# Half of the first product of blocks 4 to 10 as seven smaller products

## The chip, the cores and the metric

The kernel runs on one core of a Trainium2 chip. The metric is the device time of one execution in microseconds (us), the median over the runs of a kernel. Engines: TensorE (PE) multiplies matrices into PSUM, and PEld is its loading of weights. VectorE (DVE), ScalarE (ACT) and GpSimd (POOL) work on elements. SyncE (SP) issues the DMAs of this kernel, all on one queue.

## The reference

A retention recurrence (RetNet) over 4 batches, 8 heads, 768 steps and a head size of 64, then a feed-forward layer with the activation mish on the 3072 tokens that it gives, 512 wide, 2048 inside:

```python
for t in range(S):
    state = gamma[None, :, None, None] * state + np.einsum('bhd,bhe->bhde', k[:, :, t], v[:, :, t])
    y[:, :, t] = scale * np.einsum('bhd,bhde->bhe', q[:, :, t], state)
...
x = np.ascontiguousarray(y.transpose(0, 2, 1, 3)).reshape(B * S, H * D)
h = x @ w_in
sp = np.where(h > 20.0, h, np.log1p(np.exp(np.minimum(h, 20.0))))
g = h * np.tanh(sp)
out = (g @ w_out).astype(np.float32)
```

Inputs and output are float32. The kernel multiplies in 16-bit floats and adds up in 32 bits.

## The kernel before

**Chunks and blocks.** The tokens are cut into 24 chunks of 128 (6 per batch). Block 0 has four chunks, blocks 1 to 10 have two (256 tokens). A block goes through the recurrence in its chunked form, which gives `xts[blk]`, the transposed x in 16 bits (4 groups of 128 channels by tokens), then through the feed-forward layer.

**First product.** `g1(blk, u)` for u = 0 to 7 makes two of the 16 groups of 128 hidden channels: 2 times 4 matmuls of 128x128 weights (`wins`) against 256 tokens into one PSUM bank, and one `AF.Mish` of 512 elements per partition on ACT into the tile `g` (`gtiles`).

**Second product.** `seven(blk, ...)` multiplies the block's 2x2 parts of g with the 2x2 parts of w_out by seven products instead of eight (Winograd's form of Strassen's scheme). The sums of weights (`tmats`) are made once. `sums_a`, `sums_b` and `sums_c` make the sums of g (`gsums`) on DVE in each block. Each of the seven products is 8 matmuls of 256 columns. ACT copies three results out of PSUM (`snap`), DVE adds the others (`done`) into `osb`, and SP stores `osb`.

**Recurrence beside it.** In the middle of `seven`, the list `hooks[0]` calls `retain(blk + 1, blk + 2)`: PE works on the past part of y for the next block, interleaved with the scores (`at`) and outer products (`u_ps`) of the block after that, in small 64x64 matmuls, in the order of the two streams. `finish` then adds the present part and copies x out of PSUM. `settle` (three DVE steps on the states), `mask_two` (the scores times a triangular mask, on DVE) and `leave` (the state that the next block starts from) follow; in blocks 4 and up they are called after the first unit of the next block's `g1`.

**Feeding the recurrence.** q, k and v of a chunk are loaded by SP (`load_to`, three DMAs), scaled into 16 bits by POOL (`casts`: q and k into one tile, then v), and q and k are turned by a transposing DMA on SP (`turn_by_dma`). From block 3 on `cast_behind` has POOL cast the two chunks of three blocks ahead, one after the other, behind a one-element copy that waits for DVE's sums; `next_two(g, soon)` issues on SP a load, the two transposes (in block 3 both before the second load, `soon`; in later blocks one before and one after it) and a second load. The stores of a block are issued by `store_due` after units 1 and 2 of the next block's `g1`, so behind all of these in SP's order.

**Order.** The order on each engine is written out by hand and every engine runs its own list in order; semaphores hold an instruction until its operands are there and its buffer is free. PSUM has eight banks: three in the pool `mmps`, one in `pxps`, and two tiles of two banks in `atps` that hold `at` and `u_ps`.

Of the kernel before, what the change touches and what calls it, by code (L numbers as in the profile page):

```python
# [9 lines left out]
FP16 = mybir.dt.float16  # L10
FP32 = mybir.dt.float32
AF = mybir.ActivationFunctionType
ALU = mybir.AluOpType
# [3 lines left out]
def kernel(  # L17
# [102 lines left out]
    gtiles, tmats, gsums = {}, [], []  # L120
    ONE = 3
    nload, ncast = [0], [0]
    stores, weight_left = [], []

# [64 lines left out]
    def store_due(now):  # L191
        while stores and stores[0][0] <= now:
            _, dst, osb = stores.pop(0)
            nc.sync.dma_start(dst, osb)
# [165 lines left out]
            nc.vector.tensor_copy(dst, src)  # L360

    def casts(g):
        qf, kf, vf = loaded.pop(g)
        qk16 = castp.tile([P, 2, H, D], FP16, name="qk16", bufs=4)
        q16, k16 = qk16[:, 0], qk16[:, 1]
        v16 = castp.tile([P, H, D], FP16, name="v16", bufs=7)
        heads = slice(g % 2 * (H // 2), (g % 2 + 1) * (H // 2))
        nc.gpsimd.tensor_tensor(  # L368
            q16.rearrange("p (r h) d -> p h r d", r=2), qf,
            qs_two[:, heads].unsqueeze(3).broadcast_to((P, H // 2, 2, D)), op=ALU.mult)  # L370
        nc.gpsimd.tensor_tensor(  # L371
            k16, kf, boosts.unsqueeze(2).broadcast_to((P, H, D)), op=ALU.mult)
        nc.gpsimd.tensor_tensor(  # L373
            v16, vf, vs[g % 2].unsqueeze(2).broadcast_to((P, H, D)), op=ALU.mult)
        cast[g] = (q16, k16, v16, qk16)

    def turn_by_dma(g):
        qkt = qktp.tile([P, H, C], FP16, name="qkt", bufs=6)
        nc.sync.dma_start_transpose(qkt, cast[g][3].rearrange("p a h d -> p (a h d)"))
        qkts[g] = (qkt[:, :HP].rearrange("p (r i) c -> p i r c", r=2), qkt[:, HP:])  # L380

    def cast_to(g):
        while ncast[0] < min(g, NCK):
            casts(ncast[0])
            ncast[0] += 1
# [100 lines left out]
    def settle(blk):  # L486
        a = first[blk]
        u = held[blk][1]
        for j in range(2):
            us[a + j] = u[:, :, j]  # L490
        mid_of(a)
        state_of(a)
        mid_of(a + 1)

    def mask_two(blk):
        at = held.pop(blk)[0]
        am = tpp.tile([P, 2, 2, HP, D], FP16, name="am")
        nc.vector.tensor_tensor(  # L498
            am.rearrange("p a j i c -> p (a j i) c"), at.rearrange("p a j i c -> p (a j i) c"),
            tri_half.rearrange("p r c -> p (r c)").unsqueeze(1).broadcast_to((P, 4 * HP, D)), op=ALU.mult)  # L500
        for j in range(2):
            ams[first[blk] + j] = am[:, :, j]

    def leave(blk):
        state_of(first[blk] + 1)
# [128 lines left out]
    def sums_a(blk, half):  # L634
        n = NFB // 4
        (s1, s2, _, _), a11, _, a21, a22 = sum_views(blk, slice(half * n, (half + 1) * n))
        nc.vector.tensor_tensor(s1, a21, a22, op=ALU.add)  # L637
        nc.vector.tensor_tensor(s2, s1, a11, op=ALU.subtract)
# [5 lines left out]
    def sums_c(blk):  # L644
        (_, s2, _, s4), _, a12, _, _ = sum_views(blk)
        nc.vector.tensor_tensor(s4, a12, s2, op=ALU.subtract)  # L646

    def seven(blk, masks, hooks, last):
        n, hf = NFB // 2, d_model // 2
        px = pxps.tile([P, hf], FP32, name="o_ps", tag="px")  # L650
        pb = mmps.tile([P, hf], FP32, name="o_ps", tag="mm")
        osb = [op.tile([P, d_model], FP32, name="osb", tag="osb") for _ in range(2)]

        def a(i, j):
            return lambda f: gts[blk, j * n + f][:, i * P:(i + 1) * P]

        def b(i, j):
            return lambda f: wouts[(i * n + f) // FPS][:, f % FPS, j * hf:(j + 1) * hf]

        def s(i):  # L660
            return lambda f: gsums[blk % 2][:, i - 1, f]

        def t(i):
            return lambda f: tmats[(i - 1) // 2][:, (i - 1) % 2, f]

        def mm(o_ps, x, w, first=False):
            for f in range(n):
                nc.tensor.matmul(  # L668
                    o_ps, x(f), w(f), start=first and f == 0, stop=f == n - 1,
                    skip_group_check=True)  # L670

        def snap(o_ps):
            x = op.tile([P, hf], FP32, name="snap", tag="snap", bufs=3)
            nc.scalar.copy(x, o_ps)  # L674
            return x

        def done(i, j, o_ps, plus=None):
            dst = osb[i][:, j * hf:(j + 1) * hf]
            if plus is None:
                nc.vector.tensor_copy(dst, o_ps)  # L680
            else:
                nc.vector.tensor_tensor(dst, o_ps, plus, op=ALU.add)  # L682
            if last:
                nc.sync.dma_start(out_rows(blk, i)[:, j * hf:(j + 1) * hf], dst)

        mm(px, a(0, 0), b(0, 0), True)
        m1 = snap(px)
        mm(pb, a(0, 1), b(1, 0), True)
        done(0, 0, pb, m1)
        sums_b(blk)  # L690
        if blk == 1 or not tight(blk):
            cast_behind(blk, 2)
        for fn, *args in masks:
            fn(*args)
        pe = mmps.tile([P, hf], FP32, name="o_ps", tag="mm")
        if last:
            mm(px, s(2), t(2))
            u2 = snap(px)
        mm(pe, s(1), t(1), True)
        m5 = snap(pe)  # L700
        if not last:
            mm(px, s(2), t(2))
            u2 = snap(px)
        for fn, *args in hooks[0]:
            fn(*args)
        sums_c(blk)
        if blk > 1 and tight(blk):
            cast_behind(blk, 3)
        for fn, *args in hooks[1]:
            fn(*args)  # L710
        mm(px, s(3), t(3))
        done(1, 1, px, m5)
        for fn, *args in hooks[2]:
            fn(*args)
        mm(pe, s(4), b(1, 1))
        done(0, 1, pe, u2)
        mm(px, a(1, 1), t(4))
        done(1, 0, px)
        if not last:
            for i in range(2):  # L720
                stores.append((1 + i, out_rows(blk, i), osb[i]))
# [180 lines left out]
    def turn_next(g):  # L902
        if g < NCK:
            cast_to(g + 1)
            turn_by_dma(g)
# [2 lines left out]
        turn_next(g)  # L908
        load_to(g + 3)

    def next_two(g, soon):
        load_to(g + 3)
        turn_next(g)
        if soon:
            turn_next(g + 1)
        load_to(g + 4)
        if not soon:
            turn_next(g + 1)

    def cast_behind(blk, i):  # L920
        g = first[blk] + (6 if blk == 1 else 8)
        if ncast[0] < min(g, NCK):
            nc.gpsimd.tensor_copy(summed, gsums[blk % 2][:, i, NFB // 2 - 1, P - 1:])  # L923
            cast_to(g)

    def tight(blk):

        return blk <= ONE

    def plan_of(blk):  # L930
        a = first[blk] + 4
        plan = {u: [] for u in (0, 1, 4, 5, 7)}
        if tight(blk):
            plan[5] = [(get_ready, blk + 1)]
        elif blk + 1 < len(BLOCKS):
            plan[0] = [(settle, blk + 1), (mask_two, blk + 1), (leave, blk + 1)]
        if blk == 1:
            plan[0] += [(turn_next, a)]
            plan[1] += [(load_to, a + 3)]
        elif blk < ONE:  # L940
            plan[1] += [(next_chunk, a)]
            plan[4] += [(load_to, a + 4)]
        return plan

    first_block()
    for blk in range(1, len(BLOCKS)):
        last = blk + 1 == len(BLOCKS)
        plan = plan_of(blk)
        for u in range(NFB // 2):
            store_due(u)  # L950
            g1(blk, u)
            if u in ((6, 7) if tight(blk) else (5, 7)):
                sums_a(blk, u // 7)
            for fn, *args in plan.get(u, ()):
                fn(*args)
            if weight_left:
                weight_left.pop(0)()
        hooks = [[], [], []]
        if not last:
            later = blk + 2 if ONE <= blk < len(BLOCKS) - 2 else None  # L960
            hooks = [[(retain, blk + 1, later, True)],
                     [(next_two, first[blk] + 6, tight(blk))] if blk >= ONE else
                     [(turn_next, first[blk] + 5), (load_to, first[blk] + 8)] if blk == 1 else
                     [(next_chunk, first[blk] + n) for n in (5, 6, 7)],
                     [(finish, blk + 1)] if later is None else []]
        if tight(blk):
            hooks[2].append((leave, blk + 1))
        seven(blk, [(mask_two, blk + 1)] if tight(blk) else [], hooks, last)
# [31 lines left out]
```

## Time and profile before

| What | Before |
|---|---|
| Runs | 201.29, 201.52 and 685.0 us; median 201.52 |
| Profiled execution | 201.44 us, of which the span of the program's instructions is 199.7 us |
| Granted PE clock | 1.000 |
| PE busy | 192.4 us of the span (96%) |
| DVE, ACT, POOL busy | 111.6, 92.1, 74.8 us (56%, 46%, 37%) |
| DMA queue of SP | 82.0% of the 16 engines' span |
| Blocks 4 to 9, first matmul to first matmul | 14.71, 14.71, 14.71, 14.52, 14.59, 14.31 us |

The busy share of PE is an average. Which engine the others wait for is read from the chain of waits, in which each piece of work is followed back to what released it, and from the timeline: what one engine's list holds around a given moment. The starts of the blocks 4 to 10 lie at 95.86, 110.57, 125.28, 139.99, 154.51, 169.10 and 183.41 us of the span.

### The profile page before, as it was taken

What the parts mean: (1) busy time and instruction counts of PE and PEld (TensorE: products, weight loads), DVE (VectorE), ACT (ScalarE), POOL (GpSimd) and SP (SyncE); (2) the same over time, 40 slices, a digit from 0 to 9 for tenths busy, and PEclk for the clock granted to TensorE, in tenths of its full rate; (3) what the DMA queues carried; (4) which work ended last, traced back from release to release, by engine and by line L of the source; (5) the groups of instructions that cost most, each with busy time, mean ns of one, the idle gap of its engine ahead of it and who ended that gap; (6) DMA issues with size and microseconds to landing.
All of it is one profiled execution on the core that took longest, in us unless ns stands there. A gap on an engine that the chain in (4) does not pass through costs nothing.

```text
span 199.7 us, 6553 instructions
## 1 busy us (share of the span) xinstructions
PE 192.4 (96%) x2871; PEld 155.1 (78%) x2871; DVE 111.6 (56%) x204; ACT 92.1 (46%) x166; POOL 74.8 (37%) x93
## 2 busy tenths in 40 slices
PE   7887999999999999999999999999999999999993
PEld 7765444445888888888888888888888888888882
DVE  0688444997359169266836745545753654455052
ACT  2376773242542542554454454454553553642640
POOL 6562000669807603942907508409409300000000
PEclk9999999999999999999999999999999999999999
DMA  5999999999999999999999999996932600201102
GB/s 180 300 316 356 390 382 343 316 254 214 239 232 250 188 214 271 127 215 211 258 155 300 194 232 202 199 225 126 206 121 40 175 3 11 98 3 54 56 26 79
DMA packets 83612, 38.74 MB, mean 194 GB/s; under 512 B 57728, under 2 KB 77696, under 8 KB 83584
## 3 DMA queue, kind: packets, MB, share of 16 engines
q1 hardware_dynamic: 83440, 38.28, 82.0%
q8 instruction: 22, 0.36, 0.8%
q10 hardware_dynamic: 144, 0.05, 0.2%
q14 instruction: 6, 0.05, 0.1%
HBM read 27.31 MB, written 6.29 MB: 168 GB/s over the span
## 4 chain that ended last, share of the span: by engine, by line
PE 69%; DMA 16%; SPq 7%; DVE 3%; POOL 2%; issue 1%; DVEq 0%; POOLq 0%
PE h_ps L576 33%; PE o_ps L668 31%; DMA wi<-in_moe_w_in_dram 5%; DMA wt<-in_moe_w_out_dram 5%; SPq L243 3%; PE y_ps L509 3%; DMA qf<-in_q_dram 3%; DMA qkt<-qk 3%; SPq L160 2%; PE at L421 2%; PE u_ps L428 1%; POOL qk L368 1%; POOL qk L371 1%; DVE win L177 1%; DVE wout L188 1%
## 5 line engine op out<-in xcount | busy, mean ns | idle before, releaser
L576 PE MATMUL h_ps<-xt,win 128*128 128x256 f16 (+1 forms) x704 | 86.0, 282 | 0.8 <-ACT xt L358 0.7
L576 PEld LDWEIGHTS <-win 128*128 128x128 f16 x704 | 68.5, 98 | 16.0 <-POOL win L177 0.9
L584 ACT ACTIVATE g<-h_ps 128x512 f16<-128x512 f32 x96 | 57.3, 597 | 48.3 <-PE h_ps L576 48.3
L668 PEld LDWEIGHTS <-gsum 128*128 128x128 f16 x320 | 30.1, 98 | 4.5 <-DVE gsum L646 0.7
L668 PE MATMUL o_ps<-tmat,gsum 128*128 128x256 f16 x240 | 29.4, 273 | 0.0
L668 PEld LDWEIGHTS <-g 128*128 128x128 f16 x240 | 23.5, 98 | 2.7
L637 DVE TENSOR_TENSOR gsum<-g 128x512 f16<-128x512 f16 x20 | 8.6, 429 | 28.4 <-ACT g L584 28.4
L674 ACT COPY snap<-o_ps 128x256 f32<-128x256 f32 x30 | 11.2, 372 | 21.5 <-PE o_ps L668 21.5
L368 POOL TENSOR_TENSOR qk<-qf,qvs 128x512 f16<-128x512 f32 x18 | 19.5, 1086 | 3.6 <-DMA qf<-in_q_dram 2.5
L373 POOL TENSOR_TENSOR v<-vf,qvs 128x512 f16<-128x512 f32 x18 | 20.7, 1148 | 0.0
L923 POOL COPY summed<-gsum 128x1 f16<-128x1 f16 x7 | 1.3, 187 | 51.7 <-DVE gsum L642 36.9
L371 POOL TENSOR_TENSOR qk<-kf,qvs 128x512 f16<-128x512 f32 x18 | 20.1, 1118 | 0.0
L682 DVE TENSOR_TENSOR osb<-o_ps,snap 128x256 f32<-128x256 f32 x30 | 12.7, 424 | 12.4 <-PE o_ps L668 7.4
L668 PE MATMUL o_ps<-wout,g 128*128 128x256 f16 x160 | 19.1, 273 | 0.0
L563 ACT CAST xt<-y_ps 128x512 f16<-128x512 f32 x15 | 10.2, 733 | 11.3 <-PE y_ps L509 11.3
L590 PE MATMUL o_ps<-wout,g 128*128 128x512 f16 x64 | 15.0, 380 | 0.0
L465 DVE TENSOR_TENSOR mid<-u_ps,sth 128x256 f16<-128x256 f32 x15 | 6.3, 422 | 10.1 <-PE u_ps L428 9.8
L498 DVE TENSOR_TENSOR am<-at,tri_half 128x1024 f16<-128x1024 f32 x9 | 10.9, 1216 | 0.0
L590 PEld LDWEIGHTS <-g 128*128 128x128 f16 x64 | 5.8, 97 | 6.6
L668 PE MATMUL o_ps<-wout,gsum 128*128 128x256 f16 x80 | 10.4, 274 | 0.0
L668 PE MATMUL o_ps<-tmat,g 128*128 128x256 f16 x80 | 10.4, 273 | 0.0
L392 PE MATMUL at<-ident 128*128 128x128 f16 (+1 forms) x79 | 8.0, 276 | 1.4 <-POOL ident L96 1.4
(77 smaller groups left out, 184.0 us busy)
## 6 DMA issues: line engine op xcount, KB each, us to landing
kf<-in_k_dram SPq DMA_DIRECT2D x24, 256.0 KB, 4.8
vf<-in_v_dram SPq DMA_DIRECT2D x24, 256.0 KB, 5.3
out_dram<-osb SPq DMA_DIRECT2D x22, 256.0 KB, 3.9
qf<-in_q_dram SPq DMA_DIRECT2D x20, 256.0 KB, 4.1
wt<-in_moe_w_out_dram SPq DMA_DIRECT2D x3, 1024.0 KB, 9.8
wi<-in_moe_w_in_dram SPq DMA_DIRECT2D x4, 512.0 KB, 8.5
wi<-in_moe_w_in_dram SPq DMA_DIRECT2D x2, 1024.0 KB, 10.6
qfirst<-in_q_dram SPq DMA_DIRECT2D x2, 512.0 KB, 4.6
```

The lines of the kernel that those rows point to most:

```text
L368: nc.gpsimd.tensor_tensor(q16.rearrange("p (r h) d -> p h r d", r=2), qf, qs_two[:, heads].unsqueeze(3).broadcast_to((P, H // 2, 2, D)), o ...
L371: nc.gpsimd.tensor_tensor(k16, kf, boosts.unsqueeze(2).broadcast_to((P, H, D)), op=ALU.mult)
L373: nc.gpsimd.tensor_tensor(v16, vf, vs[g % 2].unsqueeze(2).broadcast_to((P, H, D)), op=ALU.mult)
L498: nc.vector.tensor_tensor(am.rearrange("p a j i c -> p (a j i) c"), at.rearrange("p a j i c -> p (a j i) c"), tri_half.rearrange("p r c -> ...
L563: nc.scalar.copy(dst[:, :, :, s], src)
L576: nc.tensor.matmul(h_ps[:, j], wins[s][f // 2][:, bp, f % 2 * P:(f % 2 + 1) * P], xts[blk][:, bp, :nt], start=(bp == 0), stop=(bp == NBP - 1))
L584: nc.scalar.activation(gt, h_ps, AF.Mish, scale=inv_boost3)
L590: nc.tensor.matmul(o_ps, gts[blk, fb][:, t * P:(t + 1) * P], wouts[s][:, f, cols], start=(fb == 0), stop=(fb == NFB - 1))
L637: nc.vector.tensor_tensor(s1, a21, a22, op=ALU.add)
L668: nc.tensor.matmul(o_ps, x(f), w(f), start=first and f == 0, stop=f == n - 1, skip_group_check=True)
L674: nc.scalar.copy(x, o_ps)
L682: nc.vector.tensor_tensor(dst, o_ps, plus, op=ALU.add)
```

## The change

From block 4 on, `g1` is replaced by `mixed_in`. Of the 16 groups of hidden channels, eight (0 to 3 and 8 to 11) come from seven products of half the depth and half the width: each is 8 matmuls of 128x128 weights against 128 tokens. The other eight groups (`plain`) are made as before, in four pairs. The sums of input weights that this takes (`in_sums`, tiles `wsum`) are made once by DVE, four operations in each of blocks 2 and 3. The sums of x (`x_sums`, four DVE operations on 128x256) are put into the free right half of the xt tile at the end of `seven` of the block before, two before and two after its last output copies. In `mixed_in`, ACT copies three partial results to SBUF (`kept`), DVE adds three (`plus`), and Mish of these three reads the sum from SBUF. One PSUM tile of the plain pairs is taken from `atps`.

`settle` and `mask_two` are called after the third group of products in `mixed_in`, `leave` near its end, and the sums of g (`sums_a`) at the end. In `seven` the second product runs over its second half first (`turn`). On POOL, `cast_behind` now casts only q and k of the first of two chunks; q and k of the second, and both v, are cast by `second_of` at the start of the next block, behind a one-element copy that waits for the last sum of x. On SP, `next_two` issues the first transpose between the two loads, in every block; `second_of` issues the second one, after the stores of the block (`store_due(NFB)` is called just before it).

```diff
     def casts(g):
-        qf, kf, vf = loaded.pop(g)
+        casts_qk(g)
+        casts_v(g)
+
+    def casts_qk(g):
+        qf, kf, _ = loaded[g]
...
+    def in_sums(j):
+        t = cpool.tile([P, 4, 2, TB // 2], FP16, name=f"wsum_{j}")
+        wsums.append(t)
+        (a11, a12), (a21, a22) = [(x[:, :2], x[:, 2:]) for x in (wins[0][j], wins[2][j])]
+        sub = ALU.subtract
+        return [
+            lambda: nc.vector.tensor_tensor(t[:, 0], a21, a22, op=ALU.add),
+            lambda: nc.vector.tensor_tensor(t[:, 1], t[:, 0], a11, op=sub),
+            lambda: nc.vector.tensor_tensor(t[:, 2], a11, a21, op=sub),
+            lambda: nc.vector.tensor_tensor(t[:, 3], a12, t[:, 1], op=sub),
+        ]
...
+    def x_sums(blk, part):
+        ((b11, b12), (b21, b22)), t = x_views(blk)
+        sums = ((t[0], b12, b11), (t[1], b22, t[0]), (t[2], b22, b12), (t[3], b21, t[1]))
+        for to, a, b in sums[2 * part:2 * part + 2]:
+            nc.vector.tensor_tensor(to, a, b, op=ALU.subtract)
+
+    def mixed_in(blk, last):
...
+        def mm(o_ps, w, x, begin=False):
+            for f in range(n):
+                for k in range(2):
+                    nc.tensor.matmul(
+                        o_ps[:, f], w(f // 2, k)[:, f % 2 * P:(f % 2 + 1) * P], x[:, k],
+                        start=begin and f == 0 and k == 0, stop=k == 1, skip_group_check=True)
...
+        pp = bank(mmps, "mm", True)
+        pf = bank(mmps, "mm")
+        pa = bank(mmps, "mm")
+        mm(pa, a(0, 0), b[0][0], True)
+        m1 = kept(pa)
+        plain(pp, n)()
+        mm(pf, s(1), t[0], True)
+        m5 = kept(pf)
+        if not last:
+            settle(blk + 1)
+            mask_two(blk + 1)
+        plain(bank(pxps, "px", True), n + 2)()
+        pm = bank(mmps, "mm")
+        mm(pm, a(0, 1), b[1][0], True)
+        h11 = plus(pm, m1)
+        mm(pa, s(2), t[1])
+        u2 = kept(pa)
+        mish(part(0, 0), h11)
+        mm(pf, s(4), b[1][1])
+        h12 = plus(pf, u2)
+        mish(part(0, 1), h12)
+        plain(bank(pxps, "px", True), 3 * n)()
+        mm(pa, s(3), t[2])
+        h22 = plus(pa, m5)
+        mish(part(1, 1), h22)
+        if not last:
+            leave(blk + 1)
+        sums_a(blk, 0)
+        ph = atps.tile([P, 2, 2, 2 * C], FP32, name="h_ps", tag="at")[:, 0]
+        plain(ph, 3 * n + 2)()
+        mm(pa, a(1, 1), t[3])
+        mish(part(1, 0), pa)
+        sums_a(blk, 1)
...
-        mm(pb, a(0, 1), b(1, 0), True)
+        mm(pb, a(0, 1), b(1, 0), True, n // 2 if blk > ONE else 0)
...
+        mixes = not last and blk >= ONE
+        if mixes:
+            x_sums(blk + 1, 0)
         mm(pe, s(4), b(1, 1))
         done(0, 1, pe, u2)
         mm(px, a(1, 1), t(4))
         done(1, 0, px)
+        if mixes:
+            x_sums(blk + 1, 1)
...
-    def next_two(g, soon):
+    def next_two(blk):
+        g = first[blk] + 6
         load_to(g + 3)
-        turn_next(g)
-        if soon:
-            turn_next(g + 1)
+        if g < NCK:
+            turn_by_dma(g)
         load_to(g + 4)
-        if not soon:
-            turn_next(g + 1)
+
+    def second_of(blk):
+        g = first[blk] + 6
+        if g < NCK:
+            nc.gpsimd.tensor_copy(summed, xts[blk + 1][:, 3, TB - 1:])
+            casts_qk(g + 1)
+            turn_by_dma(g + 1)
+            casts_v(g)
+            casts_v(g + 1)
...
             nc.gpsimd.tensor_copy(summed, gsums[blk % 2][:, i, NFB // 2 - 1, P - 1:])
-            cast_to(g)
+            if blk >= ONE:
+                cast_to(g - 2)
+                casts_qk(g - 2)
+                ncast[0] = g
+            else:
+                cast_to(g)
...
-        elif blk + 1 < len(BLOCKS):
-            plan[0] = [(settle, blk + 1), (mask_two, blk + 1), (leave, blk + 1)]
...
-        for u in range(NFB // 2):
+        if blk > ONE:
+            store_due(NFB)
+            second_of(blk - 1)
+            mixed_in(blk, last)
+        elif blk > 1:
+            weight_left.extend(in_sums(blk - 2))
+        for u in range(NFB // 2 if blk <= ONE else 0):
             store_due(u)
             g1(blk, u)
```

## The prediction

> **What bounds the kernel now.** I read the busy table first, then the chain of waits and the table by windows over blocks 4 to 10, the only ones that get `mixed_in`.
>
> ```profile
> PE 192.4 (96%) x2871; PEld 155.1 (78%) x2871; DVE 111.6 (56%) x204; ACT 92.1 (46%) x166; POOL 74.8 (37%) x93
> ```
>
> ```profile
> 95.86 6.99 PE h_ps L576 x64
> 102.85 3.49 PE o_ps L668 x32
> ```
>
> ```profile
> 95.86:110.57 14.71, 14.70 (x243) 12.86 (x241) 9.09 (x17) 7.22 (x13) 8.43 (x10) 1.00 1.15 236
> 169.10:183.41 14.31, 14.31 (x186) 12.50 (x185) 7.74 (x16) 6.62 (x12) 0.00 (x0) 1.00 0.10 38
> ```
>
> A block is 14.3 to 14.7 us and PE is busy in all of it (second column; then weight loads, DVE, ACT, POOL, clock, DMA share). 6.99 us of it is the first product, on the path: 64 matmuls at 0.109 us start to start. DVE has 5 to 7 us free in a block and ACT 7. The DMA share is 1.15 in block 4 and 0.10 in block 9: early in this stretch the DMA engines have a backlog, which decides one of my terms.
>
> **The products.** `mixed_in` has 32 matmuls of 256 columns and 56 of 128. No row has the short ones against changing weights in this place; the nearest are PE's transposes, which load new weights for each, and the identity matmuls.
>
> ```profile
> 1.36 4.89 PE L392 MATMUL at<-ident 128*128 128x128 f16 x46 [1.36 <-POOL ident L96]
> 6.21 0.62 PE L215 MATMUL t_ps<-ident,qk 128*128 128x128 f16 x8
> 6.67 0.94 PE L392 MATMUL at<-ident 128*128 128x128 f16 x14
> ```
>
> One takes 0.22 to 0.27 us and they overlap: (0.62 - 0.22) / 7 = 0.056 us start to start, (0.94 - 0.27) / 13 = 0.052. The first 46 are at 0.106: PE starts slow. I take 0.056, as it changes weights: 32 x 0.109 + 56 x 0.056 = 3.49 + 3.14 = 6.63 us, 0.36 less than 6.99 per block (0.5 with 0.053).
>
> The Trainium skill speaks against this ("TensorE: Matmul & The Clock Gate", section "Back-to-back issue gap"): a sustained stream of weight load and matmul at 128 columns is given as about 81 ns each. By that, 56 x 0.081 = 4.54 and each block would lose 1.04 us; the transposes here are at 56 ns.
>
> **The chain through ACT and DVE.** Seven groups need a copy or a sum before PE may use their bank again. Durations:
>
> ```profile
> L584 ACT ACTIVATE g<-h_ps 128x512 f16<-128x512 f32 x96 | 57.3, 597 | 48.3 <-PE h_ps L576 48.3
> L682 DVE TENSOR_TENSOR osb<-o_ps,snap 128x256 f32<-128x256 f32 x30 | 12.7, 424 | 12.4 <-PE o_ps L668 7.4 <-ACT xt L563 3.3 <-ACT snap L674 1.0
> L498 DVE TENSOR_TENSOR am<-at,tri_half 128x1024 f16<-128x1024 f32 x9 | 10.9, 1216 | 0.0
> L642 DVE TENSOR_TENSOR gsum<-g 128x1024 f16<-128x1024 f16 x10 | 6.8, 682 | 0.0
> ```
>
> `kept` is as Mish, 0.60 us; `plus` on 512 lies between 0.424 (256) and 1.216 (1024): 0.69. An x sum of 256 in 16 bits is 0.29 (0.42 for 512, 0.68 for 1024). ACT's successive operations overlap by 0.1 us:
>
> ```profile
> 15.42 1.06 ACT L358 CAST xt<-y_ps 128x512 f16<-128x512 f32 x2
> ```
>
> (two of 0.58 in 1.06). PE's end to ACT's start takes 0.20 us, to DVE's 0.25, the release of PE 0.05. I walk the lists from the block's first matmul. PE ends the groups at 0.45, 1.32, 1.77, 2.64, 3.09, 3.54, 3.99, 4.86 and 5.31 us. DVE: last output copy to 0.62, two x sums to 1.04, `settle` to 2.29, mask to 3.42, h11 3.34 to 4.03, h12 (waits for u2, copied by 4.33) 4.38 to 5.07, h22 5.56 to 6.25. The last short group needs h22's bank: PE has 5.31 + 0.87 = 6.18 us of work, so it waits 0.12 and ends at 6.75. ACT's last five Mish run at 5.12, 5.62, 6.30, 6.80, 7.30, ending at 7.90; `turn` lets PE need the last at 8.06. So a block gains 6.99 - 6.75 = 0.24 us; with ACT's overlap gone the last Mish ends 0.2 later and 0.1 is left; with 0.053 and ACT in time, 0.4. The two x sums ahead of the block's end lie in DVE's wait for the last products (0.64 us in block 4). Seven blocks: -1.7 us (-0.5 to -2.9).
>
> `settle` and the mask move later by 0.4 us, `leave` by 3.3; `retain` needs them at 10. Next in their line is the bank of `at`, free at 3.42 where `ph` takes it at 5.31. Were the mask 2 us later, PE would wait.
>
> **POOL and the sums of input weights.** In blocks 2 and 3 DVE idles 5 us before `settle`, so four `wsum` of 0.42 are hidden there, even at twice that. But POOL casts at that time, and a DVE sum between two SBUF tiles collides with it: L646 is 0.68 alone and 1.59 beside POOL (107.01), whose cast takes 1.49 instead of 1.04. Four times 0.45 makes the last transpose of block 3 up to 1.8 us later; PE uses it at 92.1, some 5.5 us after its issue at 86.6, against the 3.1 to 6.1 us to landing shown below. I put +0.3 (0 to 1.5).
>
> **The second transpose of block 3.** This is the moved step. `next_two(3)` issued both transposes, then a load, and the stores came after. Now SP's order is transpose, load, two stores, transpose. Rows of before for these pieces, and the use:
>
> ```profile
> 96.91 5.19 SPq L379 DMA_TRANSPOSE qkt<-qk  x2
> 102.15 0.62 SPq L143 DMA_DIRECT2D qf<-in_q_dram  x1
> 104.06 1.82 SPq L194 DMA_DIRECT2D out_dram<-osb  x2
> 106.65 0.23 PE L421 MATMUL at<-qkt 64*64 64x64 f16 x4
> 108.07 3.87 SPq L379 DMA_TRANSPOSE qkt<-qk  x1
> ```
>
> ```profile
> DMA to landing us min/median/max: 3.1/4.7/6.1
> ```
>
> One transpose behind three loads keeps SP 3.87 us (full queues), three loads 1.91 (102.15 to 104.06), two stores 1.87. The second transpose is issued at 96.91 + 3.87 + 0.05 + 1.91 + 1.87 = 104.6, in place of about 100.9; its casts, behind the x sums, end near 99. It lands at 107.7, 109.3 or 110.7 by the three figures. PE's scores of that chunk stand in block 4's `seven`, at 106.65 - 0.24 = 106.4. I take the median, as loads and stores are ahead: PE waits 2.9 us (1.3 to 4.3). Behind it wait the present part of y, ACT's x copies and two thirds of `seven`. What PE gets back is its wait for s4:
>
> ```profile
> PEld L668 <- DVE gsum L646: 0.7, 3, 0.3
> ```
>
> 0.3 us in block 4, as `sums_c` then runs clear of POOL. In blocks 5 and 6 the casts of the second chunk end 3.4 us after the block's start, the stores are issued by 5, the transpose lands by 8 to 9.5 and is used at 10.4: 1 to 2 us to spare, no term. Both v are cast by 5.5 and used at 10; the loads behind the transpose on SP are for chunks of two blocks later, and their buffers are free by then. If that spare time is gone, each of three blocks waits up to 1 us.
>
> **Sum.** Against the profiled execution of 201.44 us (span 199.7): -1.7 + 0.3 + 2.9 - 0.3 = +1.2, so 202.6. The median of the runs is 0.1 above that execution: 202.7 us.
>
> **Rivals.** *A, the transpose is there in time.* The DMA backlog drains before 104.6 or the queue takes it at once; for it, an unloaded transpose keeps SP 1.2 us and lands in 3.1; against it, the share of 1.15 in this window. Without wait: 201.5 - 1.7 = 199.8 us, and the moved order costs nothing.
>
> *B, PE comes out of the wait slow.* The 46 matmuls at 0.106 show PE at half pace for 4.9 us after idling; no idle stretch of 2.9 us in this trace shows whether that one does it. Price 4.9 / 2 = 2.4 us: 205.1. The Trainium skill (same page, section "Part 1: The HAM clock gate (the "warmup" mystery)") has the clock halved after an idle window of about 3.4 us, which the 2.9 us would not fill and 4.3 would; no row here shows it.
>
> *C, slower: the short products go at the pace of weight loading.* In `mixed_in` each of the 56 has its own load; a load's row has a mean of 98 ns. If they do not overlap, 56 x (0.098 - 0.056) = 2.35 us more per block, times seven 16.5: 219 us. A block stops gaining at 0.056 + 0.24 / 56 = 0.060 us each, and the kernel passes +4 us at 0.056 + 2.8 / 392 = 0.063. Against it, the transposes, which start every 0.056 with loads of 98 ns. At the 81 ns of the page cited above it would be 202.7 + 392 x 0.025 = 212.5.
>
> **Chances and range.** Forecast 0.55, A 0.22, B 0.12, C 0.11. About what a measurement of this kernel can tell from no change is 2% (4 us). Faster by that needs more than the 0.5 us per block that the columns give: 0.03, from A with luck. Slower: C, half of B and the long landing, 0.20. Within: 0.77. Range: A with its larger gain, 199.2, to B with some of the longer waits, 206.0; C is left out.
>
> **What would show it.** A short group of 8 should start 0.45 us before the next, `mixed_in` take 6.75 us, and blocks 5 to 9 be 0.24 us shorter each. In block 4 the scores should wait for `qkt`, 2 to 3 us, near 106.5. I am wrong if that wait is absent (A), if PE's 256-column matmuls after it are at 0.21 (B), or if short groups take 0.55 or more (C). Waits of PE on `hsum` or on Mish of over 0.3 us per block would break the walk.

## The result, and the profile after

The changed kernel takes 203.3 to 206.1 us, against 201.3 to 202.2 for the kernel before in the same measurement: ratio 1.013, 95% interval 1.008 to 1.018, so a little slower and inside the 2% of "no change"; the forecast's ratio, 1.006, lies below that interval. The profiled execution takes 203.9 us with a span of 201.3 us and a granted clock of 1.00; before it was 201.44 and 199.7. So 1.6 us were added inside the span and 0.8 around it. The predicted 202.7 us has the right sign and half of the size: +1.2 us forecast for this execution, +2.5 measured. 206.0 was the range's end, and the longest executions pass it.

The busy table of the changed kernel, then its chain of waits in block 4 (start us, us, engine, tile, line, count):

```profile
PE 189.9 (94%) x3039; PEld 154.5 (77%) x3039; DVE 139.2 (69%) x261; ACT 101.4 (50%) x187; POOL 75.2 (37%) x98
```

```profile
97.12 0.45 PE h_ps L689 x8
97.57 0.87 PE h_ps L709 x8
98.44 0.45 PE h_ps L689 x8
...
103.30 0.52 PE h_ps L689 x8
103.81 0.88 PE o_ps L782 x8
...
104.72 4.08 DMA qkt<-qk
108.80 0.04 issue
108.84 0.22 PE at L427 x2
```

PE has 2.5 us less to do and 168 matmuls more. The first product runs from 97.12 to 103.81: 6.69 us where it took 6.99. Each short group (L689) takes 0.45 us, that is 0.056 per matmul, and only the last one holds a wait, of 0.07. Then the chain leaves PE for the second transposition of block 3 and comes back at 108.84.

The table by windows for blocks 4 and 9 (length; busy time of PE, weight loads, DVE, ACT, POOL; clock; DMA share; GB/s), and the waits of PE (us in total, times, longest):

```profile
97.12:112.60 15.48, 14.41 (x268) 13.01 (x265) 10.87 (x26) 8.61 (x16) 6.40 (x8) 1.00 1.14 233
171.03:185.05 14.02, 14.02 (x212) 12.50 (x209) 10.54 (x23) 7.92 (x15) 0.00 (x0) 1.00 0.10 39
```

```profile
PE at L427 <- DMA qkt<-qk: 2.3, 3, 1.1
...
PE o_ps L782 <- DVE xt L676: 1.0, 1, 1.0
```

Block 9 is 0.29 us shorter than before and PE is never idle in it. Block 4 is 0.77 longer: 1.07 of its 15.48 us are idle, the wait on `qkt`. The second row of waits, on an x sum, was not foreseen. It is one place, in block 6, between the products with s3 and with s4, two of the seven, each with a sum of g (timeline: PE, and what DVE does meanwhile):

```profile
138.51 1.05 PE L782 MATMUL o_ps<-tmat,gsum 128*128 128x256 f16 x8
140.60 0.61 PE L782 MATMUL o_ps<-wout,gsum 128*128 128x256 f16 x4 [1.05 <-DVE xt L676]
```

```profile
137.98 1.46 DVE L652 TENSOR_TENSOR gsum<-g,gsum 128x1024 f16<-128x1024 f16 x1
139.65 0.42 DVE L796 TENSOR_TENSOR osb<-o_ps,snap 128x256 f32<-128x256 f32 x1 [0.21 <-ACT xt L569]
140.15 0.62 DVE L676 TENSOR_TENSOR xt<-xt 128x256 f16<-128x256 f16 x2
```

In the program the products with s4 wait for the sum L652, which ends at 139.44. PE starts 1.16 us later. The x sum only happened to end near that time; the profile names the last event that it saw. So the stand had no cause yet.

The balance by blocks, from the traces (the length of a block runs from its first matmul to that of the next, block 10 to the last matmul; "start" is that of block 2, as the timeline gives it, 0.16 us ahead of the chain's time). All kernels below are in it:

```text
kernel             start    2     3     4     5     6     7     8     9    10   span  ratio to before
before             64.95 15.08 15.67 14.71 14.71 14.70 14.53 14.58 14.31 13.26 199.7
after              65.56 15.08 16.32 15.48 14.41 15.51 14.23 14.28 14.01 12.97 201.3 1.013 [1.008, 1.018]
a_again            65.25 15.08 16.16 15.58 14.41 15.90 14.36 14.29 14.00 12.97 202.9 1.011 [1.005, 1.017]
e1_sp_order        65.03 15.12 16.09 14.41 15.05 15.35 14.23 14.28 14.01 12.97 200.0 1.002 [0.998, 1.006]
e2_sums_early      66.08 15.08 15.67 20.01 14.41 15.04 14.29 14.29 14.01 12.96 205.1 1.013 [1.007, 1.019]
e3_both            66.03 15.08 15.68 14.41 15.32 14.73 14.30 14.29 14.01 12.97 200.0 1.000 [0.998, 1.002]
f1_rows_152        67.07 15.09 16.06 16.12 14.41 14.41 14.23 14.29 14.01 12.96 202.1 1.013 [1.011, 1.016]
f2_order_rows      66.83 15.08 16.36 14.41 14.41 14.41 14.22 14.29 14.01 12.97 200.4 1.009 [1.005, 1.014]
f3_both_rows       71.85 15.08 15.86 14.41 15.32 14.41 14.23 14.28 14.01 12.97 205.6 1.006 [1.004, 1.009]
f4_rows_48         69.93 15.08 15.67 18.49 15.29 14.85 14.23 14.28 14.01 12.97 208.2 1.037 [1.032, 1.042]
g1_rows_136        72.24 15.08 16.30 18.22 14.41 14.41 14.23 14.28 14.02 12.96 209.6 1.039 [1.032, 1.047]
g2_repaired        70.67 15.08 16.37 14.41 15.04 14.42 14.22 14.29 14.01 12.97 204.8 1.027 [1.024, 1.029]
g4_before_rows     72.30 15.08 15.87 14.71 15.35 14.71 14.52 14.59 14.31 13.26 207.9 1.041 [1.037, 1.044]
k1_repaired_late   68.84 15.08 15.76 14.41 14.41 14.41 14.23 14.29 14.01 12.96 201.6 1.008 [1.005, 1.011]
```

The ratios leave out executions that took over 1.5% longer than the fastest of their kernel at a lowered clock: one of four of the changed kernel (206.7 us), eight of ten of `f2`, so that its ratio rests on two, and among others the profiled ones of `e2`, `f3` and `g1`. After against before, in us: +0.61 ahead of block 2, +0.65 in block 3, +0.77 in block 4, +0.81 in block 6, -0.29 to -0.30 in each of the other five, +0.3 behind the last matmul: +1.6. The +0.61 I take for chance: a transposition that PE uses near 55.5 us landed at 56.23 here and at 55.92 in `a_again`, the same kernel (55.62 before).

### The profile page after: what moved, and what is told of

It reads as the page before. It is cut to its first block, busy times and chain, and to the rows that moved or that the text cites. A ratio compares the mean times of both kernels' runs of the same rounds, so it can differ in the third digit from the quotient of the medians.

```text
span 201.3 us, 7009 instructions
## 1 busy us (share of the span) xinstructions
PE 189.9 (94%) x3039; PEld 154.5 (77%) x3039; DVE 139.2 (69%) x261; ACT 101.4 (50%) x187; POOL 75.2 (37%) x98
## 4 chain that ended last, share of the span: by engine, by line
PE 60%; DMA 20%; POOL 7%; SPq 7%; DVE 2%; issue 2%; ACT 0%; POOLq 0%; DVEq 0%; ACTq 0%
PE o_ps L782 27%; PE h_ps L709 12%; PE h_ps L689 11%; DMA qkt<-qk 7%; DMA wi<-in_moe_w_in_dram 5%; DMA wt<-in_moe_w_out_dram 5%; PE h_ps L582 4%; SPq L243 3%; DMA qf<-in_q_dram 3%; PE y_ps L515 3%; POOL qk L375 2%; POOL v L380 2%; SPq L160 2%; POOL qk L372 2%; PE at L427 2%
## 5 line engine op out<-in xcount | busy, mean ns | idle before, releaser
L582 PE MATMUL h_ps<-xt,win 128*128 128x256 f16 (+1 forms) x256 | 36.0, 299 | 0.8 <-ACT xt L358 0.7
L590 ACT ACTIVATE g<-h_ps 128x512 f16<-128x512 f32 x40 | 23.9, 597 | 19.5 <-PE h_ps L582 19.5
L582 PEld LDWEIGHTS <-win 128*128 128x128 f16 x256 | 24.6, 98 | 11.0 <-POOL win L177 0.9
L709 PE MATMUL h_ps<-xt,win 128*128 128x256 f16 x224 | 29.0, 273 | 0.0
L782 PEld LDWEIGHTS <-g 128*128 128x128 f16 x240 | 23.2, 98 | 2.6
L709 PEld LDWEIGHTS <-win 128*128 128x128 f16 x224 | 20.7, 98 | 1.9
L700 ACT ACTIVATE g<-h_ps 128x512 f16<-128x512 f32 x35 | 19.9, 588 | 3.3 <-PE h_ps L709 3.3
L719 ACT COPY hsum<-h_ps 128x512 f32<-128x512 f32 x21 | 12.3, 585 | 16.2 <-PE h_ps L689 16.2
L380 POOL TENSOR_TENSOR v<-vf,qvs 128x512 f16<-128x512 f32 x18 | 19.5, 1097 | 1.1 <-DMA vf<-in_v_dram 1.1
L724 DVE TENSOR_TENSOR hsum<-h_ps,hsum 128x512 f32<-128x512 f32 x21 | 14.5, 691 | 7.3 <-PE h_ps L689 5.5
L689 PE MATMUL h_ps<-xt,wsum 128*128 128x128 f16 x224 | 15.9, 219 | 0.0
L689 PEld LDWEIGHTS <-wsum 128*128 128x128 f16 x224 | 14.0, 98 | 0.3
```

The costliest lines, as they stand in the source:

```text
L380: nc.gpsimd.tensor_tensor(cast[g][2], loaded.pop(g)[2], vs[g % 2].unsqueeze(2).broadcast_to((P, H, D)), op=ALU.mult)
L582: nc.tensor.matmul(h_ps[:, j], wins[s][f // 2][:, bp, f % 2 * P:(f % 2 + 1) * P], xts[blk][:, bp, :nt], start=(bp == 0), stop=(bp == NBP - 1))
L590: nc.scalar.activation(gt, h_ps, AF.Mish, scale=inv_boost3)
L689: nc.tensor.matmul(o_ps[:, f], w(f // 2, k)[:, f % 2 * P:(f % 2 + 1) * P], x[:, k], start=begin and f == 0 and k == 0, stop=k == 1, skip_g ...
L700: nc.scalar.activation(to, src, AF.Mish, scale=inv_boost3)
L709: nc.tensor.matmul(h_ps[:, f], wins[w][h // 2][:, k, h % 2 * P:(h % 2 + 1) * P], xts[blk][:, k, :2 * C], start=k == 0, stop=k == NBP - 1)
```

## The experiments

**The same kernel again, and the two late transpositions.** Theory 1: three waits at fixed places. `a_again` is the changed kernel unedited. `e1_sp_order` changes one thing, SP's order at the end of block 3:

```diff
     def next_two(blk):
...
-        load_to(g + 4)
+        if blk > ONE:
+            load_to(g + 4)
...
         if blk > ONE:
+            if blk - 1 == ONE:
+                second_of(blk - 1)
+                load_to(first[blk - 1] + 10)
             store_due(NFB)
-            second_of(blk - 1)
+            if blk - 1 > ONE:
+                second_of(blk - 1)
```

`e2_sums_early` changes only where the sums of the input weights are made:

```diff
-        elif blk > 1:
-            weight_left.extend(in_sums(blk - 2))
+        elif blk == 1:
+            weight_left.extend(in_sums(0) + in_sums(1))
...
-            if weight_left:
-                weight_left.pop(0)()
+            for _ in range(2 if u >= 2 else 1):
+                if weight_left:
+                    weight_left.pop(0)()
```

`e3_both` has both edits.

> The changed kernel again, nothing edited. Theory 1 (the span grew by three waits of TensorE with fixed places in the program): the same three are there again: the scores of the last chunk of block 3 start at 93.3 us, block 4's scores wait 1.2 us near 107.6, and block 6 stands 1.1 us between the products with s3 and with s4 near 139.3; span 201.3, ratio 1.01. Rival 1a (the stand in block 6 comes from something that changes from run to run, such as the fetch of instructions): the first two waits are there, the third is gone or in another block, and the span is about 200.2. Rival 1b (the throttle: TensorE is slowed after a wait): a profiled execution whose granted clock is under 0.99 shows a span of 203 or more and longer products, not longer waits.

> Only the order of SP's queue at the end of block 3 is changed: the second transposition (chunk 15) is issued directly behind the first (chunk 14), ahead of the load and the two stores. GpSimd's order and all else are as in the changed kernel. Theory 1 (block 4's wait is this place in SP's queue): chunk 15 is issued near 102.5 and landed by 107, the wait of 1.2 us at 107.6 is gone, block 4 takes about 14.4 us rather than 15.48, span 200.1, ratio to before 1.002. Rival 1c (the transfer shares the DMA engines with the load behind it and is only as early as that lets it): lands at 108 or later, block 4 still waits 0.5 us or more, span 200.8 or more.

> Only the sums of the first weights (eight VectorE instructions, once) are moved, from blocks 2 and 3 to block 1, where GpSimd does little. Theory 1 (the 1.26 us ahead of block 4 are GpSimd's casts made slower by these sums): the casts of blocks 2 and 3 are back at 1.04 us, the transposition of the last chunk of block 3 is issued near 86.6 rather than 88.5, block 4 starts at 95.9 rather than 97.1; but block 4's own transposition lands no earlier, so that its scores then wait 2 to 2.5 us rather than 1.2, and the span falls by no more than 0.3: 201.0 to 201.3, ratio 1.01. Rival 2 (the casts are slow from another cause, say the output copies): block 4 starts at 97 as before.

> The sums of the first weights in block 1, and the second transposition of block 3 directly behind the first. Theory 1 (two independent lateness costs, each hidden behind the other): both waits gone, block 4 starts at 95.9 and takes 14.4 us, span 198.8 with block 6's stand of 1.1 us or 197.7 without it, time 199.5 to 200.6, ratio to before 0.990 to 0.995. Rival (TensorE pays for fewer waits with a lower clock or with other waits): span 200 or more.

Measured. In `a_again` all three waits are there: block 4 has 1.17 us idle, block 6 1.43. Its span is 202.9 where 201.3 was expected; most of that, 1.5 us, lies behind the last matmul (4.95 us there, 3.46 in the changed kernel). In `e1` the SP queue (timeline) holds both transpositions ahead of loads and stores:

```profile
97.53 4.76 SPq L385 DMA_TRANSPOSE qkt<-qk  x2
102.34 0.63 SPq L143 DMA_DIRECT2D qf<-in_q_dram  x1
...
104.27 2.38 SPq L194 DMA_DIRECT2D out_dram<-osb  x2
```

The second is issued at 101.05 and lands at 104.21 (104.72 and 108.80 in the changed kernel), and block 4 falls from 15.48 to 14.41. So that wait is the moved transposition, as theory 1 had it. But block 5 rose from 14.41 to 15.05 and block 6 kept 15.35. The span of 200.0, for 200.1 expected, is partly luck: block 4 gave 1.07 us, the time ahead of block 2 0.53 and block 3 0.23, and block 5 took 0.64.

In `e2` block 3 is back at 15.67, to the digit of before, so the 0.4 to 0.65 us there were the sums beside GpSimd's casts. POOL in the changed kernel, then in `e2`:

```profile
83.07 1.22 POOL L375 TENSOR_TENSOR qk<-kf,qvs 128x512 f16<-128x512 f32 x1
85.44 1.24 POOL L372 TENSOR_TENSOR qk<-qf,qvs 128x512 f16<-128x512 f32 x1
```

```profile
83.41 1.04 POOL L375 TENSOR_TENSOR qk<-kf,qvs 128x512 f16<-128x512 f32 x1
85.42 1.05 POOL L372 TENSOR_TENSOR qk<-qf,qvs 128x512 f16<-128x512 f32 x1
```

Block 4 of `e2` took 20.01: the moved transposition was issued at 106.15 and landed 5.5 us later, and behind that wait of 3.9 us the clock fell (below). `e3` removed both waits, and still its span is 200.0 where 198.8 was expected: block 5 took 15.32 with nothing late in it. Moving the sums also had a price ahead of block 2, which starts at 66.0 in `e2` and `e3`: in block 1 PE waits for a sum of g that VectorE now makes later (waits of PE in `e3`):

```profile
PE o_ps L782 <- DVE gsum L652: 0.4, 1, 0.4
```

Theory 1 was right for two of three waits and could not say what stands in blocks 5 and 6.

**The fetch of instructions.** The traces have another DMA queue:

```profile
q8 instruction: 23, 0.38, 0.9%
```

23 transfers, 0.38 MB: about 16.5 KB each. Set against the count of TensorE's matmuls and weight loads ("rows"), every unexplained stand ends at the same row or 512 rows further, and 1.3 to 1.6 us after one of these transfers has ended (from the traces, us):

```text
kernel          row   transfer      PE starts again   after its end
after           4286  137.84-139.14 140.60            1.46
a_again         4286  138.12-139.30 140.62            1.31
e1_sp_order     3262  109.16-110.11 111.61            1.50
e1_sp_order     3774  122.85-124.12 125.70            1.58
e1_sp_order     4286  136.50-137.80 139.29            1.49
e2_sums_early   4286  141.97-143.16 144.53            1.37
e3_both         3262  109.46-110.40 111.90            1.50
e3_both         3774  123.81-124.94 126.51            1.57
e3_both         4286  136.83-138.14 139.49            1.35
```

Theory 3: PE's program comes in pieces of 256 rows, the next one starts about when the last but one is used up, and PE stands if it is through with the 256 rows between before the piece is there. A block of `mixed_in` has 528 rows (480 before), and 256 of them can pass in 2.1 to 2.3 us, in the recurrence. This also fits the stands that `e1` gained in block 5: in the changed kernel PE, held up by `qkt` in block 4, reaches rows 3262 and 3774 some 2.3 us behind the ends of their transfers, and in `e1` 1.5 and 1.6. Test: add rows early and so shift the boundaries against the blocks. The added matmuls' results are overwritten. For the `f` kernels, n = 38 twice (24 matmuls in all for `f4`), on the changed kernel, on `e1` and on `e3`:

```diff
         spin(46, 1)
+        small(n)
         turn_first_q(qf, 0, True)
         spin(14, 1)
+        small(n)
...
+    def small(n):
+        at = pairs[min(x for x in pairs if type(x) is tuple and x[1] == "at")]
+        for _ in range(n):
+            nc.tensor.matmul(
+                at[half(0), 0, 0, 0, half(0)], ident[half(0), half(0)], ident[half(0), half(0)],
+                start=True, stop=True)
```

> The changed kernel with 76 matmuls of 64 x 64 (152 instructions of TensorE, with their weight loads) added at the start, in two places where TensorE waits for a DMA. Theory 3, formed from the first four runs: TensorE's instructions come in pieces of 256 by DMA (queue 8 of the profile); a piece is asked for when the one but one before it is used up, takes 1.0 to 1.4 us, and can be executed 1.5 us after it has come; where the 256 rows between asking and need take less than some 3 to 5 us, TensorE stands. By it the stand in block 6 (at row 4288 in every run of the changed kernel) is gone, since with 152 rows more the boundaries fall where 256 rows take 5 us or more; block 6 takes 14.4 us rather than 15.5, the two waits for transpositions stay, span 200.0 to 200.4, and the 0.85 us that the changed kernel has more around its span goes too: time 201.8 to 202.2. Rival (the stand belongs to the sums of VectorE in block 6, which is what the profile names): block 6 still takes 15.4 us or more, span 201.3.

> The same 152 rows added to the kernel with only SP's order changed (second transposition of block 3 directly behind the first). Theory 3: that kernel's excess in block 5 (15.05 us) and block 6 (15.35) was instruction fetch, and goes: blocks 4 to 6 take 14.4 each, span 198.3 to 198.7 and time 200.1 to 200.5, ratio 0.994. Rival (the earlier transposition made other work late, which stays): block 5 over 15.0 again, span 200.

> The same 152 rows added to the kernel with both repairs (sums of the weights in block 1, second transposition directly behind the first). Theory 3: block 5 takes 14.4 us rather than 15.32 and block 6 14.3 rather than 14.73, span 198.6 to 198.9, time 200.3 to 200.7, ratio 0.993 to 0.995. Rival as before: span 200.

> The changed kernel with 24 such small matmuls (48 rows) at the same places: a third of the work that the first of these adds. Theory 3: boundaries now fall at rows with 256 rows in 2.4 to 3.4 us in blocks 4 to 7, so that TensorE stands there, 2.5 to 5.5 us in all: span 202.5 to 205.5. Rival (rows at the start cost what they take, or nothing): span within 0.4 us of 201.3, and not more than that of the kernel with 152 rows by over 0.5 us.

Measured. The stands move as forecast: with 152 rows more, block 6 takes 14.41 in all three, and with `e1`'s order blocks 4, 5 and 6 are all 14.41. Block 6 of `f2`, the place where the changed kernel stood:

```profile
138.75 1.05 PE L789 MATMUL o_ps<-tmat,gsum 128*128 128x256 f16 x8
139.74 1.05 PE L789 MATMUL o_ps<-wout,gsum 128*128 128x256 f16 x8
```

0.99 us from s3 to s4, against 2.09. VectorE's sum takes 1.46 us there too, and the x sums and POOL's casts what they took, so the rival falls. With 48 rows `f4` stands at rows 3774 and 4286, 1.35 and 1.55 us after the transfers' ends, in other instructions of blocks 5 and 6. The whole times missed: the three spans were to be 198.3 to 200.4 and were 202.1, 200.4 and 205.6; `f4` was to be at most 205.5 and was 208.2, with a wait of 2.46 us for block 4's transposition and a lower clock behind it. At the start PE had waited only 0.66 and 0.16 us where I put the rows, and 38 take 1.39 us: what follows came 1.1 us later. A boundary at row 703 then fell into the start, where PE stood 0.8 to 3.3 us. Block 5 of `f3` (15.32) is a wait of 0.84 for a transposition that SP issued late, behind stores that held the queue for 3.1 us.

**Rows at another place, and in the kernel before.** 136 rows right ahead of block 0's first product, on the changed kernel (`g1`), on the kernel before (`g4`), and with `e1`'s order and all eight sums in block 2 (`g2`):

```diff
+        for _ in range(68 if blk == u == 0 else 0):
+            nc.tensor.matmul(
+                h_ps[half(0), 0, half(0)], ident[half(0), half(0)], ident[half(0), half(0)],
+                start=True, stop=True)
```

```diff
-        elif blk > 1:
-            weight_left.extend(in_sums(blk - 2))
+        elif blk == 2:
+            weight_left.extend(in_sums(0) + in_sums(1))
```

> The changed kernel with 68 matmuls of 64 x 64 (136 instructions of TensorE with their weight loads) put right ahead of the first product of block 0, where TensorE stands 0.7 us; they take 1.2, so 0.5 us is paid. Theory 3 (fetch of TensorE's instructions in pieces of 256): blocks 5 and 6 take 14.4 us each (14.41 and 15.51 without the rows), the waits for the two transpositions stay, span 201.3 - 1.1 + 0.5 = 200.7, and the last piece is no longer asked for at the program's end, so that 1.75 us rather than 2.6 lie around the span: time 202.4, ratio 1.005. Rival (the stand is of VectorE's sums, and the earlier runs with added rows differed by their later start): block 6 takes 15.4 or more, span 201.8.

> The changed kernel with all three repairs: second transposition of block 3 directly behind the first, all eight sums of the first weights in block 2 (one behind each of its eight groups of the first product; the last four then lie where GpSimd idles), and the same 136 rows. Theories 1 and 3: block 2 starts at 65.5 and takes 15.1, block 3 15.7, blocks 4 to 6 14.4 each, 7 to 9 14.2, 14.3, 14.0; span 198.4, time 200.1, ratio to before 0.993 (0.990 to 0.996). Rival (sums in block 2 delay VectorE's sums for its own second product): block 2 takes 15.5 or more, span 198.8 or more. Rival (there is no gain in the products once waits are gone): span 199.7 or more.

> The kernel before the change, with the same 136 rows at the same place. Theory 3: before the change the boundaries of the pieces lie, in blocks 4 to 10, where 256 rows take 4.5 us or more, by chance of the count; moved by 136 rows they lie, in blocks 4 to 7 (rows 3008, 3520, 4032, 4544), where 256 rows take 2.4 to 3.5, so that TensorE stands there, 1.6 to 5 us in all, 1.3 to 1.6 us behind the end of each such piece: span 199.7 + 0.5 + 1.6 to 5, that is 201.8 to 205.2, ratio 1.010 to 1.027. The same edit thus takes time from the changed kernel's blocks 5 and 6 and adds it here. Rival (the fetch is no bound of the kernel before): span 200.2, ratio 1.002.

Measured. In blocks 5 and 6 the forecast holds: 14.41 both in `g1`. The kernel before got the stand, in block 5 (15.35 for 14.71), at row 3774, 1.60 us behind a transfer's end (timeline of `g4`):

```profile
129.91 0.61 PE L672 MATMUL o_ps<-tmat,gsum 128*128 128x256 f16 x4
131.12 0.61 PE L672 MATMUL o_ps<-tmat,gsum 128*128 128x256 f16 x4 [0.59 <-issue]
```

There was one such stand where I expected 1.6 to 5 us of them. `g2`'s block 5 has a late transposition (0.56 us), and its block 3 stayed at 16.37 though the casts were undisturbed: chunk 13's transposition took 6.2 us to land. All three lost 5.7 to 7.4 us ahead of block 2: again a boundary at row 703, a stand from 18.0 to 21.1, and behind it a lower clock. So the spans missed by far: 209.6, 204.8 and 207.9 us, where 200.7, 198.4 and at most 205.2 were expected.

**Rows where PE waits anyway.** `k1` puts 72 tiny matmuls ahead of the scores near 55.5 us, with `e1`'s order and the sums in block 2:

```diff
+                if blk == 2 and same and fn is score and j == 1:
+                    for _ in range(72):
+                        nc.tensor.matmul(
+                            at[:16, 0, 1, 0, :16], ident[half(0), :16], ident[half(0), :16],
+                            start=True, stop=True)
```

> The changed kernel with the second transposition of block 3 directly behind the first, the eight sums of the first weights in block 2, and 72 small matmuls (16 x 16, 144 instructions of TensorE) put where TensorE waits 0.3 to 0.9 us for a transposition anyway, near 55.5 us, ahead of block 2 and behind the early pieces of instructions that the rows at the start had made late. Theory 3 with what the last runs add (a stand of over 2 us is followed by a lower granted clock, one of 1.3 us or less is not): no stand over 1 us anywhere, granted clock 1.0; block 2 starts at 65.5 to 66.0, blocks 2 and 3 take 15.1 and 15.7 to 16.1, blocks 4 to 6 14.4 each, 7 to 10 14.2, 14.3, 14.0, 13.0; span 198.7 to 199.3, time 200.5 to 201.1, ratio to before 0.994 to 0.998. Rival (block 5's transposition comes late again, as in the last repaired run): block 5 takes 15.0, span 199.3 to 199.9, ratio 0.998 to 1.0. Rival (the rows spoil another boundary between 55 and 100 us): a stand of over 1 us in blocks 2 or 3, span over 200.

Measured. From block 2 on there is no stand: 14.41 three times, then 14.23, 14.29, 14.01 and 12.96. Blocks 4 to 10 take 98.72 us, against 100.80 before and 100.89 in the changed kernel. But block 2 starts 3.9 us later: the rows came behind the wait, not in it, took 1.95 us, and the clock fell. So the span is 201.6, where 198.7 to 199.3 was expected, and no kernel here beats the one before. The best, `e3`, equals it.

## Why the prediction was right, and where it was not

**Products and the chain through ACT and DVE: right.** Forecast 0.056 us per short matmul, `mixed_in` at 6.75 us and 0.24 gained per block. Measured 0.056, 6.69 and 0.29 to 0.31 wherever nothing stands; over seven blocks -2.1 in `k1`, for -1.7. The durations taken from neighbours held (group table: busy, mean ns):

```profile
L719 ACT COPY hsum<-h_ps 128x512 f32<-128x512 f32 x21 | 12.3, 585 | 16.2 <-PE h_ps L689 16.2
L724 DVE TENSOR_TENSOR hsum<-h_ps,hsum 128x512 f32<-128x512 f32 x21 | 14.5, 691 | 7.3 <-PE h_ps L689 5.5
```

0.585 for 0.60, 0.691 for 0.69. Rival C is out: at the 81 ns that the Trainium skill gives ("TensorE: Matmul & The Clock Gate", "Back-to-back issue gap") a short group would take 0.65 us, and it takes 0.45.

**Sums beside POOL: right in kind and within its bounds.** +0.3 (0 to 1.5) forecast; 0.65, 0.49 and 0.42 in the three kernels that have them there and an unedited start, 0.00 and 0.01 in `e2` and `e3` without. In `f4`, 4.4 us later from block 2 on, they cost nothing. Nor are they all that lengthens block 3: in `f3`, `k1` and `g2`, with no sums there, it took 15.86, 15.76 and 16.37.

**The moved transposition: right in place, its wait sized too long.** Issue forecast at 104.6 (104.72), landing 4.7 us later (4.08). The wait was 1.07 us and not 2.9: block 4 itself came 1.26 us late, which the term did not subtract, and the landing took 0.6 less. In other executions of this order the wait was 1.17, 1.71, 2.34, 2.46 and 3.88 us, as landing took 3.8 to 5.5. The -0.3 for s4 shows nowhere: block 4 without waits is 14.41, like block 5. That term was misread: its row is a wait of the weight loads (PEld), and before the change PE was busy for 14.70 of block 4's 14.71 us, so nothing was there to get back.

**Rival B: the condition was right, the forecast's own case did not meet it.** Behind the waits of 1.07 and 1.71 us the clock stayed at 1.00. Behind 2.34, 2.46 and 3.88 us it fell, and block 4 lost 1.5, 1.6 and 1.7 us more than the wait, for the 2.4 that I priced: half clock lasted 3.4 us each time, and not the 4.9 of the start. This may be what separates the changed kernel's executions of 203.3 and of 206.1 us (span 203.6, clock 0.992), but no trace of the latter is there to show it.

**What failed: the step "Blocks 5 and 6 ..., no term", and the sum's offset.** Block 6 lost 0.81 instead of gaining 0.24. The list of things that could be late held buffers, banks and DMAs of data; PE's own instructions were not in it. 168 more matmuls are 336 more rows, which both thin the time per 256 rows and shift every later boundary. The 0.8 us around the span fits the same cause, by trace only: in the profiled executions of the changed kernel and `e1` the fetch of the last piece begins 1.8 and 1.7 us behind the span's end and 2.6 us lie around the span; in all others it is fetched inside it and 1.7 to 1.85 do. No experiment separated that.

So 202.7 came near by errors that cancel, and its sign is partly luck. The terms that the forecast had, as measured, are -2.1 for the products, +0.65 for the sums and +1.07 for the wait: together -0.4, a gain. The kernel is slower by what the forecast left out: 1.1 of fetch in block 6, 0.6 ahead of block 2, 0.3 behind the last matmul and 0.8 around the span. A wait sized 1.8 too long stood in their place.

## What to carry to other kernels

Count what a change adds to an engine's instruction stream, not only to its busy time: trading a few large matmuls for many small ones can pay in busy time and be given back where 256 instructions run in less than some 3 to 5 us. (That is an estimate from the stands above: a transfer starts up to 2.5 us late, takes 1.0 to 1.3, and PE goes on 1.3 to 1.6 behind it.) A profile that names a releaser which the program does not wait for is a sign to look at the instruction queue; shifting the stream by some dozens of instructions is the test. And a transposition moved behind other work on a full queue must be priced by the spread of its landing, since its worst case also takes the clock.

## What the runs showed of the hardware that I had not expected

**TensorE can starve for instructions.** About 16.5 KB per transfer, boundaries 256 rows apart, 0.9 to 1.7 us per transfer in most cases (2.4 at most), and 1.3 to 1.6 us from its end until PE goes on, in each of the stands above. What delays its start, mostly by less than 3 us behind the row that I take as its trigger (4.1 in `g1`, more near the start), is open. The Trainium skill ("Runtime: NRT & Kernel Launch", "Instruction fetch mechanics") has instructions refilled in blocks of 256 and says that this is hidden, in one place mostly hidden. The first agrees with these traces; the second does not, with 0.3 to 1.4 us per stand in blocks 5 and 6.

A block of 528 rows is two pieces and 16 rows, so a bad position comes back in the next block nearly unchanged; that is why rows 3262, 3774 and 4286 are struck in turn.

**The clock falls where PE is idle for 1.9 us of 3.41.** Windows of `e2`, of `k1` and of `f3` (length, PE busy, clock, DMA share, GB/s):

```profile
108.00:111.70 3.70, 0.00 (x0) 1.00 1.13 252
111.70:115.00 3.30, 3.29 (x87) 0.53 1.16 166
115.00:118.00 3.00, 3.00 (x32) 0.95 1.20 255
```

```profile
55.40:56.40 1.00, 0.06 (x8) 1.00 1.20 310
56.40:58.40 2.00, 2.00 (x80) 0.81 1.35 235
58.40:61.80 3.40, 3.40 (x38) 0.61 1.19 297
61.80:64.00 2.20, 2.20 (x22) 1.00 1.04 266
```

```profile
17.80:20.40 2.60, 0.04 (x7) 0.82 1.06 369
```

In `e2` PE does nothing for 3.7 us and then runs at half clock for 3.4. In `f3` the clock fell inside a stand: at a mean of 0.82, PE had full clock for 1.66 of these 2.60 us, so it fell at 19.46, 1.6 us after PE stopped. In the traces' record of the granted clock, every change lies a whole number of 3.41 us behind the clock's first rise. Among those stretches of 3.41 us, up to the last matmul, the clock fell behind each in which PE was idle for 1.9 us or more, and, `k1` apart, behind none in which it was idle for 1.6 or less. So a stand counts by how it lies to these stretches: `f1`'s of 1.71 us was cut in halves by the boundary at 109.8. In `k1` PE stood only 0.9 us, but the 2 us behind were 16x16 matmuls: busy by the record, and the clock fell all the same. The Trainium skill ("TensorE: Matmul & The Clock Gate", "Part 1: The HAM clock gate") asks for an idle window of about 3.4 us; the length agrees with the 3.41 us here, but PE need not stand through all of it: stands of 2.34 and 2.46 us were enough.
